# A program for one pattern of head flags behind a conditional: local heads score 11 blocks, and the Fourier transform stands ahead of a projection

## The chip, the cores and the metric

The kernel runs on one core of one Trainium2 chip. The metric is device microseconds of one execution, from the first to the last instruction of the program; of several runs the median counts. The core has TensorE (PE in the profile), VectorE (DVE), ScalarE (ACT), GpSimd (POOL) and SyncE (SP), which run their own instruction streams in order and wait for each other by semaphores; DMA queues move data beside them.

## The reference

Two layers follow each other. First, attention with 4 batches, 8 heads, 768 positions and 64 columns per head:

```python
scores = scale * q @ k.T                       # scale = 1/8
causal = rel >= 0                              # rel = query position - key position
stream = causal & ((key < 4) | (rel < 64))     # 4 sink keys and a window of 64
mask   = causal if is_retrieval[head] else stream
a      = softmax(where(mask, scores, -1e9))    # then a @ v
```

`is_retrieval` is an input; its value is [1, 0, 1, 0, 0, 0, 1, 0]. So heads 0, 2 and 6 are causal over everything before them ("retrieval heads") and the five others see the sink and the window alone ("local heads"). `n_sink` = 4 and `window` = 64 are known when the program is built.

Then the heads of a batch, side by side, form x (768 x 512), and a gated convolution follows:

```python
x1, x2, x3 = split(x @ w_proj, 3)              # w_proj 512 x 1536
conv = irfft(rfft(x2, axis=positions) * rfft(filter_fft, axis=positions))
out  = (x1 * conv * x3) @ w_out                # w_out 512 x 512
```

Output is 4 x 768 x 512 in float32.

## The kernel before

Work is cut into 16 pairs of heads, numbered n = 4 * batch + pair; the pair is heads 2p and 2p+1. Positions are cut into 6 tiles of 128. Names below are those of the operations in the kernel's own order; n is the pair, b the batch.

- **Loads and turns.** `lk`, `lq` and `lv` load float32; `ck`, `cq` cast q and k to bfloat16, `cv` casts v and places a column of ones beside it (`v_aug`). For n < 6 TensorE turns q and k (`T`, line 518) and `E` copies them out of PSUM; for the others a transposing DMA does it. `vf` (line 509, POOL) multiplies the values of far key tiles by a mask.
- **Scores.** A head has 21 blocks of 128 x 128 on or below the diagonal. For each pair they stand in 6 chunks (`sc`, line 542), which serve retrieval and local heads alike; the two heads of a pair use the lower and the upper 64 rows of TensorE. `ex` (line 561, ACT) takes the exponential out of PSUM. For n < 4 the mask is added in PSUM by a matmul with the identity (`sb`, line 555); for the others VectorE multiplies the exponentials by a mask (`mk`, line 571). Since the flags are data, masks and biases are made on the chip from the loaded flags (`lret`, `heads`, `code`, `mask`, `bias`, lines 350 to 388).
- **Attention.** `at` (line 580): 42 matmuls of 65 columns per pair; `rec` and `nm` (line 595) normalise; `tn`, `te` turn the result so that x stands with its columns on partitions (`xT`).
- **Convolution.** `x2` (line 633) projects; `xe`, `fa`, `fs` evict it and form the sum and the difference of the two halves of the positions (lines 645, 650); `X` (line 418) multiplies by the Fourier matrices `G`, 3 matmuls of 512 columns for each of 6 tiles; `Xe`, `pa`, `pb`, `pc` evict and multiply by the filter's spectrum (lines 664 to 674); `c` (line 716) transforms back, `ce`, `cv` (line 727) evict and join. `x1`, `x3` (line 691) project the gates, `xs`, `g`, `y` (lines 705 to 735) apply them, `o` (line 743) multiplies by `w_out`, `oe` evicts and `st` stores.
- **Order.** Nothing schedules at run time. The list `ORDER` names every operation once, with the PSUM slot (`@0` to `@3`, two banks each) that it takes and, for evictions, the engine (`/v`, `/s`, `/p` for DVE, ACT, POOL). Each engine's stream is that list, filtered.

At the start stand dummy matmuls (`blank`, line 221), and the Fourier matrices are made by sines on ACT.

## Time and profile before

Three runs took 212.41, 213.26 and 214.54 us; the median is 213.26. The profile is of one further execution:

| what | us |
|---|---|
| span of the profiled execution, its own time | 214.4 |
| PE busy | 196.3 |
| DVE busy | 177.8 |
| ACT busy | 141.9 |
| POOL busy | 58.1 |
| first exponential starts | 14.88 |
| last attention matmul ends | 169.80 |
| last eviction of the output ends | 211.08 |
| mean granted TensorE clock | 0.957 |

The profiled execution lies 1.1 us above the median of the runs and inside their spread; nothing of the program lies outside its span. Busy time counts an engine's instructions as one union of intervals. Matmuls are pipelined and their ends are modelled, so PE's busy time is longer than the pace at which it starts matmuls; the chain of work that ended last gives that pace, where PE runs without a gap. An instruction's duration on DVE and ACT overlaps the next one's by some 0.06 us.

### The profile page before, as it was taken

Reading aid. Unit: us, or ns where it says so; the run is one execution under the profiler, and the core shown is the slowest. Engines: PE = TensorE matmul, PEld = TensorE weight load, DVE = VectorE, ACT = ScalarE, POOL = GpSimd, SP = SyncE. Lnnn points to the kernel's source line nnn. Section 1 sums busy time; section 2 is a strip of 40 time slices with the busy share of each in tenths; the row PEclk is TensorE's granted clock in tenths of the full one; section 3 lists DMA queues with packets and bytes.
Section 4 is the critical chain, followed back from the end, with each engine's and each line's share of the span. In section 5 each row is a group of like instructions: output and inputs, shape, how many; then the busy total and the mean of one; then the engine's idle time right before and its main releaser. Section 6 shows DMA issues by size and latency. Waiting matters only on the chain.

```text
span 214.4 us, 4332 instructions
## 1 busy us (share of the span) xinstructions
PE 196.3 (92%) x1755; PEld 106.0 (49%) x1755; DVE 177.8 (83%) x287; ACT 141.9 (66%) x174; POOL 58.1 (27%) x79
## 2 busy tenths in 40 slices
PE   7486979899997999998999999999999999999992
PEld 2222547475355456444664564446544755555540
DVE  7379399866799879589999979999999995987951
ACT  7826785888995987996679867286779415334341
POOL 4283398066062002008534004082600000000000
PEclk9757696999999999999999999999999999999998
DMA  6799999979994047999999589999920560020436
GB/s 189 247 244 204 280 231 230 240 148 157 183 222 86 3 89 128 182 246 234 220 138 215 122 163 282 212 147 216 273 40 14 133 222 2 3 49 15 178 147 249
DMA packets 89764, 35.28 MB, mean 165 GB/s; under 512 B 80272, under 2 KB 86160, under 8 KB 89744
## 3 DMA queue, kind: packets, MB, share of 16 engines
q1 hardware_dynamic: 86848, 32.13, 67.6%
q0 software_dynamic: 2896, 2.88, 9.4%
q8 instruction: 13, 0.21, 0.4%
q14 instruction: 7, 0.06, 0.1%
HBM read 24.65 MB, written 6.29 MB: 144 GB/s over the span
## 4 chain that ended last, share of the span: by engine, by line
PE 51%; DVE 32%; ACT 7%; DMA 4%; issue 3%; POOL 1%; SPq 1%; ACTq 0%; POOLq 0%
PE x_ps L691 11%; PE out_ps L743 9%; PE x_ps L633 6%; DVE pT L571 5%; PE sc L542 5%; PE c_ps L716 5%; PE att L580 5%; ACT pT L561 4%; PE X_ps L418 4%; DMA ret_i<-in_is_retrieval_dram 4%; DVE attn L595 3%; DVE bias L382 2%; PE F_ps L418 2%; PE sc L555 2%; DVE x2s L174 2%
## 5 line engine op out<-in xcount | busy, mean ns | idle before, releaser
L561 ACT ACTIVATE pT<-sc 128x1024 bf16<-128x1024 f32 (+2 forms) x96 | 83.1, 921 | 21.6 <-PE sc L555 10.2
L691 PE MATMUL x_ps<-xT,wproj 128*128 128x384 bf16 x256 | 47.6, 326 | 2.0 <-DVE x1s L174 1.4
L542 PE MATMUL sc<-qkT 64*128 64x512 bf16 (+3 forms) x256 | 30.2, 322 | 4.9 <-DVE qkT L174 1.6
L691 PEld LDWEIGHTS <-wproj 128*128 128x128 bf16 x256 | 23.8, 98 | 21.8 <-issue 6.2
L571 DVE TENSOR_TENSOR pT<-pT,mask 128x1024 bf16<-128x1024 bf16 x37 | 31.1, 862 | 2.0 <-ACT pT L561 1.8
L493 POOL CAST qk_bf<-qk_f 128x768 bf16<-128x768 f32 x15 | 15.4, 1041 | 43.2 <-DMA qk_f<-in_q_dram 35.6
L504 POOL CAST v_aug<-v_f 128x768 bf16<-128x768 f32 x16 | 14.6, 918 | 40.7 <-DMA v_f<-in_v_dram 17.2
L580 PEld LDWEIGHTS <-pT 128*128 128x128 bf16 x672 | 23.8, 100 | 3.6 <-issue 0.9
L580 PE MATMUL att<-v_aug,pT 128*128 128x65 bf16 x352 | 24.8, 197 | 0.2 <-DVE pT L571 0.2
L743 PE MATMUL out_ps<-wout,gy 128*128 128x512 bf16 x96 | 23.2, 379 | 0.3 <-DVE gy L705 0.3
L633 PE MATMUL x_ps<-wproj,xT 128*128 128x512 bf16 x96 | 22.7, 380 | 0.0
L580 PE MATMUL att<-v_far,pT 128*128 128x65 bf16 x320 | 21.6, 196 | 0.0
L542 PEld LDWEIGHTS <-qkT 64*128 64x128 bf16 x256 | 9.6, 95 | 22.0 <-issue 15.6
L716 PE MATMUL c_ps<-Gi,P 128*128 128x384 bf16 x96 | 18.9, 326 | 1.6 <-DVE gy L705 1.3
L509 POOL TENSOR_TENSOR v_far<-v_aug,vmask 128x520 bf16<-128x520 bf16 x16 | 19.2, 1205 | 0.7
L176 ACT COPY o<-out_ps 128x1024 f32<-128x1024 f32 (+1 forms) x12 | 10.8, 911 | 10.9 <-PE out_ps L743 9.6
L418 PE MATMUL X_ps<-x,G 128*128 128x512 bf16 x72 | 18.0, 379 | 0.0
L727 DVE TENSOR_TENSOR conv<-evs,c_ps 128x384 bf16<-128x384 f32 x32 | 16.3, 548 | 1.6 <-ACT evs L176 1.3
L595 DVE TENSOR_TENSOR attn<-att,rec 128x768 bf16<-128x768 f32 x16 | 15.3, 954 | 0.6 <-DMA xT<-attn 0.2
L174 DVE COPY qkT<-qkT_ps 128x768 bf16<-128x768 bf16 x11 | 10.4, 953 | 6.2 <-PE qkT_ps L518 6.1
L176 ACT CAST x1s<-x_ps 128x768 bf16<-128x768 f32 x13 | 10.4, 805 | 7.7 <-PE x_ps L691 7.7
L176 ACT CAST x2s<-x_ps 128x1024 bf16<-128x1024 f32 x9 | 9.2, 1022 | 9.4 <-PE x_ps L633 9.0
(94 smaller groups left out, 245.9 us busy)
## 6 DMA issues: line engine op xcount, KB each, us to landing
qk_f<-in_k_dram SPq DMA_DIRECT2D x16, 384.0 KB, 6.6
qk_f<-in_q_dram SPq DMA_DIRECT2D x16, 384.0 KB, 6.3
v_f<-in_v_dram SPq DMA_DIRECT2D x16, 384.0 KB, 5.8
out_dram<-o SPq DMA_DIRECT2D x9, 512.0 KB, 3.3
wproj<-in_moe_w_proj_dram POOLq DMA_DIRECT2D x3, 512.0 KB, 7.2
out_dram<-o SPq DMA_DIRECT2D x6, 256.0 KB, 2.2
Xw<-X SPq DMA_DIRECT2D x8, 128.0 KB, 2.5
filt<-in_moe_filter_fft_dram POOLq DMA_DIRECT2D x1, 768.0 KB, 12.5
```

The costliest lines, as they stand in the source:

```text
L176: nc.scalar.copy(out=out, in_=in_)
L418: nc.tensor.matmul(ps[:, u, :], lhsT=matrix()[:, tile_no, m, :], rhs=src()[:, r, m, :], start=(m == 0), stop=(m == NM - 1))
L509: nc.gpsimd.tensor_mul(v_far(n), v_aug(n)[:, 0:4], vmask()[:, hp, :, :, None].to_broadcast([128, 4, 2, 65]))
L542: nc.tensor.matmul(sc[:, hh, m * 128:(m + cnt) * 128], lhsT=qkT(n)[rows, 1, j * 128:(j + 1) * 128], rhs=qkT(n)[rows, 0, i * 128:(i + cnt) ...
L561: nc.scalar.activation(out=pT(n)[:, :, c, 0:w], in_=held[f"sc.{n}.{c}"][:, :, 0:w], func=AF.Exp, scale=SCALE)
L571: nc.vector.tensor_mul(near, near, which)
L580: nc.tensor.matmul(att[:, hh, 65 * i:65 * i + 65], lhsT=pT(n)[:, hh, c, 128 * m:128 * m + 128], rhs=(v_far(n) if i >= j + 2 else v_aug(n)) ...
L595: nc.vector.tensor_mul(attn(n).rearrange("p i hh d -> p hh i d"), rows[:, :, :, 0:64], held[f"rec.{n}"][:, :, :, None].to_broadcast([128, ...
L633: nc.tensor.matmul(ps[:, half, :], lhsT=xT(b)[:, cc, half * HS + m * 128:half * HS + (m + 1) * 128], rhs=wproj()[:, cc, DM:2 * DM], start= ...
L691: nc.tensor.matmul(ps[:, s, 0:HS], lhsT=wproj()[:, cc, part * DM + cb * 128:part * DM + (cb + 1) * 128], rhs=xT(b)[:, cc, s * HS:s * HS + HS],
L716: nc.tensor.matmul(ps[:, r, 0:HS], lhsT=P(b)[:, t, u, ch], rhs=Gi()[:, tile_no], start=(m == 0), stop=(m == 2))
L743: nc.tensor.matmul(ps[:, i % 2, :], lhsT=gy(b)[:, cb, i * 128:(i + 1) * 128], rhs=wout()[:, cb, :], start=(cb == 0), stop=(cb == NC - 1))
```

## The change

The old program is kept whole as `general`. In front of it stands a short common part: it loads the eight flags to one partition, loads q and k of the first pair, compares the flags with one wanted pattern on VectorE, and reads the answer into a register of every engine. If the flags differ, `general` runs; otherwise a new program, `patterned`, which is built for heads 0, 2 and 6 being retrieval heads.

`patterned` differs in these ways:

- Pairs are heads c and c+4, taken in the order c = 2, 1, 0, 3. So in each batch one pair is two retrieval heads (RR), one is mixed (RL), and two are local (LL).
- A local head scores 11 blocks: 6 on the diagonal, and 5 blocks X, each of which holds the 4 sink keys and the last 64 keys of the tile before. For i = 1 that is tile 0 itself; for the others `kz`, `kx`, `ks` gather the keys, and `vx`, `vs` the values. `vf` is gone. LL has 3 chunks of scores in place of 6.
- Masks are constants (`mtab`, made by POOL), and biases one table (`btab`). The three loads of `w_proj` become six, with rows in the order of the new pairs.
- The Fourier transform is applied to the attention's output before the projection. Per pair `fd`, `fe` form difference and sum of the halves; for n >= 8 `fA`, `fS`, `fb`, `fr` go one step further, to sixths. `W` multiplies by `G` (for each of the two, 3 matmuls of 384 columns, or in sixths 2 of 256 and 1 of 128), `We` evicts 768 columns. `X` is then the projection of the transformed data: 4 matmuls of 512 columns for each of 6 tiles. `x2`, `xe`, `fa`, `fs` and the transform after the projection are gone.
- The back transform's matrices are made by TensorE (`Gt`, `Ge`), not by a DMA; q and k are turned by TensorE for n < 8; attention's outputs always (`tn`), where 7 went by DMA before. v, and q and k from n = 8, are loaded by head, in two DMAs each.
- More operations may go to any engine: `two` puts elementwise work on DVE or POOL, and `ev` can use POOL. The order is a new list, `FAST`.

The diff's core (the new order is cut, as are definitions that `patterned` repeats from `general` unchanged):

```diff
+TURNED = 8
+SIXTHS = (8, 9, 10, 11, 12, 13, 14, 15)
+TURNED_BACK = (0, 1, 2, 3, 4, 5, 6, 7, 8, 9, 10, 11, 12, 13, 14, 15)
+AHEAD = 1
+PAIRS = (2, 1, 0, 3)
+BIASED_FAST = 4
+FAST = """
+fcol0 mtab0 ck0/s lk2 lq2 ident cq0/s lq1 table tcol mblank fcol1 T0.1@0 lv0 sin0 blank2@1 angle2 E0.1/s tfrac
+mtab3 quarter lv1 turns2 T0.0 angle0 turns1 blank1@2 lk1 mtab2 E0.0/v ck2/s lq3 blank0@3 lv2 turns0 wrap2 cq2/s
...
+def _near():
+    out = []
+    for i in range(6):
+        if i:
+            out.append((0, "X", i, i, 1))
+        out.append((0, "B", i, i, 1))
+    return out
...
+SHAPES = {
+    "RR": [[[(hh, "B", j, i, cnt) for _, j, i, cnt in _runs(blocks)] for hh in range(2)] for blocks in CHUNKS],
+    "LL": [[_slot(NEAR[4 * c:4 * c + 4], hh) for hh in range(2)] for c in range(3)],
+    "RL": [
+        [_slot(NEAR[0:4], 1), [(0,) + d for d in _DIAG[0:2]]],
...
+KINDS = ("RL", "LL", "RR", "LL")
...
+    def ev(out, in_):
+        if now["engine"] == "v":
+            nc.vector.tensor_copy(out=out, in_=in_)
+        elif now["engine"] == "p":
+            nc.gpsimd.tensor_copy(out=out, in_=in_)
+        else:
+            nc.scalar.copy(out=out, in_=in_)
+
+    def two(out, a, b, op):
+        (nc.gpsimd if now["engine"] == "p" else nc.vector).tensor_tensor(out, a, b, op)
...
+            @op(f"vx{n}")
+            def _(n=n, which=which):
+                ev(v_x(n)[64:128, :, which], v_aug(n)[64:128, 1:5, which])
...
+            @op(f"kx{n}")
+            def _(n=n, at=at):
+                ev(kx(n)[at, :, 64:128], qkT(n)[at, 1].rearrange("r (n c) -> r n c", c=64)[:, 3:10:2])
...
+        @op(f"fd{n}")
+        def _(n=n):
+            x = attn(n).rearrange("p i hh d -> p i (hh d)")
+            two(fo(n)[:, 0], x[:, 0:NM], x[:, NM:NT], ALU.subtract)
...
+                if n in SIXTHS:
+                    nc.tensor.matmul(ps[:, u, 0:256], lhsT=br(n)[:, 1, u], rhs=G()[:, 3 * u:3 * u + 2, 0],
+                                     start=True, stop=False)
+                    nc.tensor.matmul(ps[:, u, 0:256], lhsT=uv(n)[:, 1 + 2 * u], rhs=Gk()[:, u],
+                                     start=False, stop=True)
+                    nc.tensor.matmul(ps[:, u, 256:384], lhsT=br(n)[:, 0, u], rhs=G()[:, 3 * u + 2, 0],
+                                     start=True, stop=True)
+                else:
+                    for m in range(NM):
+                        nc.tensor.matmul(ps[:, u, 0:HS], lhsT=fo(n)[:, u, m], rhs=G()[:, 3 * u:3 * u + 3, m],
+                                         start=(m == 0), stop=(m == NM - 1))
...
+                    for cc in range(NC):
+                        nc.tensor.matmul(ps[:, u, :], lhsT=xh(b)[:, cc, chain, 128 * part:128 * part + 128],
+                                         rhs=wproj()[:, cc, DM:2 * DM], start=(cc == 0), stop=(cc == NC - 1))
...
+    nc.sync.dma_start(out=flags, in_=is_retrieval[None, :])
...
+    nc.vector.tensor_scalar(out=zeros, in0=flags.bitcast(I32), scalar1=0.0, scalar2=None, op0=ALU.is_equal)
+    nc.vector.tensor_mul(local, zeros[:, 0:2 * H:2], zeros[:, 1:2 * H:2])
+    nc.vector.tensor_tensor(differs, local, want, ALU.not_equal)
+    nc.vector.tensor_reduce(out=other, in_=differs, op=ALU.max, axis=mybir.AxisListType.X)
+    reg = nc.values_load(other[0:1, 0:1], min_val=0, max_val=1)
+    with tc.If(reg != 0, preferred_fallthrough_block=False) as cmp:
+        general(tc, ahead, q, k, v, is_retrieval, n_sink, window, moe_w_proj, moe_filter_fft, moe_w_out, out)
+    with cmp.Else():
+        patterned(tc, ahead, pre, q, k, v, int(n_sink), int(window), moe_w_proj, moe_filter_fft, moe_w_out, out)
```

In the built program `patterned` stands directly behind the branch, `general` behind `patterned`, and the closing barrier behind `general`; so every engine jumps over `general` at the end.

## The prediction, made before the changed kernel was run

> **What bounds the kernel now.** First the page's list of engines:
>
> ```profile
> PE 196.3 (92%) x1755; PEld 106.0 (49%) x1755; DVE 177.8 (83%) x287; ACT 141.9 (66%) x174; POOL 58.1 (27%) x79
> ```
>
> PE looks full. The second view, the page's chain of work that ended last, puts less of the span on it:
>
> ```profile
> PE 51%; DVE 32%; ACT 7%; DMA 4%; issue 3%; POOL 1%; SPq 1%; ACTq 0%; POOLq 0%
> ```
>
> So two engines share the bound. Third, the table of windows, cut at the first exponential and at the last attention matmul:
>
> ```profile
> 0.00:14.88 14.88, 10.67 (x47) 4.45 (x47) 8.98 (x21) 8.44 (x13) 6.94 (x24) 0.78 0.79 230
> 14.88:169.80 154.92, 145.01 (x1488) 80.26 (x1487) 136.15 (x210) 119.01 (x143) 51.13 (x56) 0.97 0.91 175
> 169.80:214.41 44.61, 40.61 (x224) 21.34 (x222) 32.70 (x58) 14.45 (x19) 0.00 (x0) 0.99 0.31 105
> ```
>
> After the window and its length come PE, PEld, DVE, ACT, POOL. There are three stages: a head of 14.9 us; a middle of 154.9 in which DVE is busy 88%; a tail of 44.6. Fourth, the chain in order of time shows what carries the tail (start, us, what):
>
> ```profile
> 182.51 1.94 PE X_ps L418 x9
> ...
> 190.30 3.25 PE x_ps L691 x20
> 193.55 2.59 PE out_ps L743 x12
> 196.14 1.95 PE c_ps L716 x12
> ```
>
> The tail is PE without a gap, and it gives PE's true prices: 0.216 us for 512 columns, 0.163 for 384 (3.25/20, 1.95/12).
>
> **PE, part by part.** By such prices the old program's matmuls cost 170 us, dummies left out: attention's 672 at 0.0305 (1.28 us for 42) are 20.5; scores 17.1 (the chain has 8 matmuls, three chunks for both heads, in 0.60 us, so 0.05 per pair of blocks, times 336); biases 5.4; `x2` and `X` 36.3 (168 of 512 columns); the rest is unchanged or small.
> - Scores: 16 x (21 + 11) / 2 = 256 pairs of blocks, -4.0. The trace doesn't show how 128-column matmuls of two heads overlap: nearest rows are 0.05 a pair if they do and 0.07 a matmul if they don't (4.6 us for 64), up to +6 for the 252 of them. I take the first, since the long ones overlap fully.
> - Attention 472 matmuls for 672: -6.1. Biases (18 x 128, 5 x 384, 10 x 512 columns): -1.4.
> - `X` is 96 x 0.216 = 20.7, and the transform ahead 12.1 (48 x 0.163, and 16 sets of 0.27): 32.8 for 36.3, -3.5. Filter 24 to 18 matmuls: -1.3.
> - Transposes at 0.057 to 0.073: q and k +24, results +42, `Gt` 18: +4.9. They replace 10 DMA transposes, so DMA, 91% busy in the middle, is relieved. Loads by head add 32 issues of 0.45 us to SP's queue and `w_proj` three of 0.79 to POOL's; I cost SP's at nothing, since it mostly waits for buffers. Without that cover v would come late, and `cv` and `at` with it.
>
> PE: 170 - 11 = 159.
>
> **ACT.** Exponentials: 44 x 0.99, 16 x 0.82, 4 x 0.60 and 4 small, 61 for 86. Evictions and casts moved to it (9 `E` for 1, 11 casts for 5, 6 of v, 11 `We` for 9 `xe`, 5 more `ce`, 5 more `te`), a third table load (1.28) and `nm5` as 12 small ones: +37. ACT goes from 142 to 154.
>
> **DVE.** Removed, by the groups' busy time: mask and bias tables 15; `fa`, `fs`, `x2` evictions 14; mask products 31 to 23 (28,032 columns for 37,888); moved elsewhere (`ce`, 4 `E`, 7 `y`, filter scaling and others) 20. Added: `fd`, `fe` and the sixths 12; `We` 5; `kx`, `vx`, `v_aug` 8; constants, flags, other evictions 7. 178 - 57 + 32 = 153.
>
> To that comes POOL. The timeline of the two engines (start, us, instruction):
>
> ```profile
> 95.72 0.69 DVE L571 TENSOR_TENSOR pT<-pT,mask 128x1024 bf16<-128x1024 bf16 x1
> ...
> 99.64 1.53 DVE L571 TENSOR_TENSOR pT<-pT,mask 128x1024 bf16<-128x1024 bf16 x1
> ```
> ```profile
> 98.16 1.28 POOL L493 CAST qk_bf<-qk_f 128x768 bf16<-128x768 f32 x1
> 99.40 1.22 POOL L509 TENSOR_TENSOR v_far<-v_aug,vmask 128x520 bf16<-128x520 bf16 x1
> ```
>
> The same product takes 0.69 us alone and 1.53 beside POOL's. Over all groups DVE's times exceed their undisturbed ones by 17 us, for 49 us of POOL work on SBUF: 0.35 us each. The new POOL work is 60 us: 15 `fd`/`fe` of 384 and 9 gate products of 768 columns at `v_far`'s 2.0 ns a column, 3 of 1024, 13 of 256, 15 copies for v, 14 casts. At 0.35 that is 21, of which 9 are in the 153: DVE becomes 165. Between 153 (no extra) and 177 (the 0.55 of the 97 to 101 us stretch, 2.1 us lost in 3.8) I take the mean rate, since the new POOL operations are as long as the old (about 0.9 us).
>
> The Trainium skill (SBUF — State Buffer, Who interferes with whom) says that the port which the two engines share goes to one instruction for its whole length and the other engine's waits. The trace agrees (0.69 against 1.53). By that rule a DVE operation that reads PSUM with one SBUF input stays free, and the 0.94 to 0.96 us of every `nm` beside POOL bear it out.
>
> **Head.** Before the branch only the flags and two loads are issued; everything else on all engines stands behind the register. No row has a register load or a branch. Above, the bound is the old flags' load, 8.0 us from issue to landing; below, 0.8, when the engines start now. I take 5: a load lands after about 2.2 (shortest row of DMA issues) from 0.8, four small DVE operations of 0.2, and 1 us for register and branch. This delays the second pair's loads by some 3 us. Then ACT, in order: three table loads 3.8, four casts 3.3, `turns` 1.8, three `E` 2.5, sines 2.9: 14.4, and 1.5 of waits on loads and PE's 17 dummies. First exponential at **21** (14.9 before), 17 to 25 by the bounds. What hid the old setup, waits for loads, no longer hides this.
>
> **Tail.** Behind the last attention matmul PE still has 18 gate projections of four (11.7), `X` 5.2, 12 back transforms (5.9), two batches of `o` (10.4), `W` and transposes 2.3: **35.5** for 40.7. DVE has about 26 there, ACT 13. Then 3.9 us for the last eviction, store and barrier, as now, and one jump over `general`: instruction fetches show as 13 packets on the page, 1.07 us each; the store's landing (2.2) hides part. I take 1.1, between 0 and 3: **5.0**.
>
> The Trainium skill (Runtime: NRT & Kernel Launch, Instruction fetch mechanics) says that a taken branch to a far target stalls for a fetch of that block. No run here shows it; by it the jump costs, and the fall into `patterned` doesn't.
>
> **Middle.** DVE 165 - 9.5 (head) - 26 (tail) = 129.5. It filled 88% of the old middle, and 96% of 130 to 170 us (38.50 of 40). PE has 119, ACT 128, both level with it, which speaks against 96%: I take 91%, **142.5**. The ends, 135 and 147 to 155, make the range.
>
> **Sum.** 21 + 142.5 + 35.5 + 5.0 = 204 against the profiled 214.4. The runs' median is 0.5% under that execution, so **203** against 213.26.
>
> **Rivals.**
> - **ACT becomes the bound.** It gains 12 us while the others lose, and its stream has evictions on which PE's four slots wait. For: the middle's ACT load is 154 - 13 - 13 = 128, and it filled only 77% (119.0 of 154.9). At 84%: 152, sum 213.5, median **212.4**, no change. Against: its idle time now is mostly waiting on PE. Chance 0.12.
> - **POOL's port makes it slower.** Place: mask products and spectrum products of the middle, with POOL's gate and sum operations beside them. At 0.55 us of DVE per us of POOL: DVE 177, middle (177 - 35.5)/0.91 = 155.5, and at the old 88% 161: 217 to 222, median about **218**. It decides from 0.5 on, where the middle is 153. For: stretches like 97 to 101 us. Against: the mean is 0.35. Chance 0.13.
> - **The pattern isn't recognised**, and `general` runs: 214.4 + 5 + 1, median **219**. Flags 0, 2, 6 are what `want` holds. Chance 0.01.
> - **The forecast**, 195 to 210: chance 0.74.
>
> From these: faster by over 1% 0.76, within 1% 0.11, slower by over 1% 0.13; 1% is about what a measurement of this kernel can tell from none. Range for 8 in 10: 195 to 214, which takes in DVE's better filling, a head of 25 us and the ACT case.
>
> **What would show it.** First exponential near 21 us; the branch done near 5. Exponentials 61 us, ACT busy near 154, DVE near 165, POOL near 70, PE's tail near 35 us without gaps. Mask products beside POOL longer than 1 us mean the lock; mean ratios over 1.6 the slower rival. A head beyond 25 us, score matmuls of 128 columns above 0.07, or idle DVE waiting for ACT's `E` and `We` in the middle would make the number wrong.

## The result and the profile after

The changed kernel takes **206.63 us** in the median of six executions (205.25 to 210.22), the kernel before 213.9 in the median of six: ratio **0.965**, 95% interval 0.958 to 0.972. A ratio here and below counts only executions within 1.5% of the quickest of their kernel; medians are of all. The profiled execution has a span of 205.4 us, against 214.4 before. Forecast were 203 (195 to 214) and, for the span, 204. Time and span are not the same: over all executions on record the time is 1.4 to 3.3 us longer than the span (207.14 for the 205.4 here). The profiled execution of the kernel before, with its span of 214.4, was therefore longer than its three first runs and not inside their spread; the medians differ by 7.3 us where the two profiles differ by 9.0.

The engines in the page of the changed kernel, busy us, share of the span and instructions:

```profile
PE 183.4 (89%) x1718; PEld 107.1 (52%) x1718; DVE 161.0 (78%) x296; ACT 143.8 (70%) x199; POOL 81.5 (40%) x106
```

TensorE loses 13 us and VectorE 17, ScalarE gains 2, GpSimd 23. The chain of work that ended last, by engine:

```profile
PE 63%; ACT 16%; DVE 15%; issue 2%; DMA 1%; ACTq 0%; DVEq 0%
```

Before, it was PE 51% and DVE 32%. VectorE's share has halved; what that is worth is asked below. The windows, cut as before at the first exponential and at the last attention matmul (length, then PE, PEld, DVE, ACT, POOL, granted clock, DMA share, GB/s):

```profile
0.00:18.88 18.88, 10.28 (x67) 5.53 (x68) 10.22 (x29) 13.29 (x18) 10.58 (x28) 0.98 0.96 278
18.88:163.91 145.03, 137.04 (x1444) 82.11 (x1444) 121.97 (x223) 117.06 (x162) 57.24 (x68) 0.97 0.75 166
163.91:205.42 41.51, 36.04 (x211) 19.44 (x207) 28.77 (x46) 13.50 (x19) 13.68 (x12) 0.96 0.24 85
```

So the head costs 4.0 us more (18.9 for 14.9), the middle 9.9 less (145.0 for 154.9), the tail 3.1 less (41.5 for 44.6): 9.0 in all. In the middle TensorE has 8.0 us less to do than before (137.0 for 145.0), VectorE 14.2 less (122.0 for 136.2). TensorE is busy 94% of the middle in both kernels, VectorE 88% before and 84% now.

Each pair of heads has one reciprocal (`rec`), which dates the progress of the attention. The sixth starts at 69.3 us in both profiles, so all of the 9.0 us arise behind it. The stretch from the sixth to the last reciprocal, first of the kernel before, then of the changed one:

```profile
69.28:169.95 100.67, 97.66 (x951) 53.27 (x950) 91.36 (x140) 76.41 (x94) 24.77 (x23) 1.00 0.86 162
69.30:163.96 94.66, 91.46 (x933) 54.27 (x933) 88.60 (x171) 74.72 (x100) 35.01 (x39) 1.00 0.63 145
```

It is 6.0 us shorter, and TensorE has 6.2 us less to do in it. TensorE is busy 97% of it in both kernels; VectorE's share rises, from 91% to 94%.

The middle of the changed kernel is not one stage. A finer cut shows it:

```profile
55.00:79.62 24.62, 21.89 (x213) 12.07 (x210) 20.76 (x35) 19.62 (x34) 6.84 (x7) 1.00 0.71 148
79.62:144.75 65.13, 64.35 (x656) 38.03 (x657) 59.88 (x117) 52.05 (x70) 23.56 (x28) 1.00 0.70 155
144.75:153.61 8.86, 8.76 (x89) 4.66 (x88) 8.51 (x18) 7.88 (x10) 3.86 (x4) 1.00 0.06 19
```

From 79.6 to 144.8 us TensorE is busy 99% of the time and VectorE 92%; then for nine us VectorE is 96% busy, and TensorE still 99%. The chain in order of time names one of the two nearly full engines at each moment. Two cuts of it (start, us, what), the first from the long stretch, the second from the nine us:

```profile
101.81 1.28 PE f_att L1449 x42
103.09 0.34 PE f_xt_ps L1522 x6
103.42 3.45 PE f_X_ps L1553 x16
106.88 0.88 PE f_sc L1385 x7
...
146.80 0.95 DVE f_attn L1466
147.98 0.69 DVE f_m L974
```

Apart from two ScalarE steps (84.8 to 85.8 and 88.9 to 89.8 us) the chain is PE from 79.6 to 144.8, with attention, transposes and `X` back to back at 0.0305 (1.28/42), 0.057 and 0.216 (3.45/16) us each. From 144.8 to 153.6 it leads through ScalarE (1.5 us) and then VectorE. That doesn't make VectorE alone the bound there: in the same nine us TensorE started its matmuls without a gap of more than 0.1 us, so both engines were full. The tail looks alike. Its chain leads through ScalarE and VectorE in places, but the window row below it shows TensorE busy nearly throughout:

```profile
168.76 0.37 DVE f_uv L974
169.13 0.47 DVE f_conv L1629
169.65 3.42 PE f_x_ps L1588 x20
...
189.58 0.48 ACT f_evs L971
190.12 0.49 ACT f_evs L971
190.65 1.14 PE f_c_ps L1618 x6
...
200.28 0.59 ACT f_o L971
```
```profile
163.91:200.28 36.37, 36.04 (x211) 19.44 (x207) 28.77 (x46) 12.91 (x18) 13.68 (x12) 1.00 0.21 74
```

Between 163.9 and 200.3 us some 5.7 us of the chain are evictions and joins on ScalarE and VectorE (up to 166.5, 167.6 to 169.65 and 189.6 to 190.65). TensorE had other work in that time: by the starts of its matmuls under 1 us of the 36.4 is lost.

### The profile page after: what moved, and what is told of

Read it like the earlier page. It is cut to its first block, busy times and chain, and to the rows that moved or that the text cites. A ratio compares the mean times of both kernels' runs of the same rounds, so it can differ in the third digit from the quotient of the medians.

```text
span 205.4 us, 4423 instructions
## 1 busy us (share of the span) xinstructions
PE 183.4 (89%) x1718; PEld 107.1 (52%) x1718; DVE 161.0 (78%) x296; ACT 143.8 (70%) x199; POOL 81.5 (40%) x106
## 4 chain that ended last, share of the span: by engine, by line
PE 63%; ACT 16%; DVE 15%; issue 2%; DMA 1%; ACTq 0%; DVEq 0%
PE f_x_ps L1588 15%; PE f_X_ps L1553 10%; PE f_out_ps L1645 9%; PE f_c_ps L1618 7%; PE f_sc L1385 6%; ACT f_pT L1404 5%; PE f_att L1449 4%; PE f_blank_ps L1010 3%; DVE f_attn L1466 3%; PE f_qkT_ps L1340 2%; ACT f_qkT L971 2%; DVE f_fo L974 2%; ACT f_HAB L1205 2%; PE f_xt_ps L1522 2%; PE f_W_ps L1510 2%
## 5 line engine op out<-in xcount | busy, mean ns | idle before, releaser
L1404 ACT ACTIVATE f_pT<-f_sc 128x1024 bf16<-128x1024 f32 (+3 forms) x68 | 59.8, 921 | 7.2 <-PE f_sc L1385 5.1
L1588 PE MATMUL f_x_ps<-f_xT,f_wproj 128*128 128x384 bf16 x256 | 48.3, 327 | 1.0 <-ACT f_pT L1404 0.5
L1588 PEld LDWEIGHTS <-f_wproj 128*128 128x128 bf16 x256 | 23.1, 98 | 17.7 <-issue 2.6
L1385 PE MATMUL f_sc<-f_qkT 64*128 64x128 bf16 (+3 forms) x248 | 23.1, 258 | 1.9 <-DVE f_attn L1466 0.9
L1645 PE MATMUL f_out_ps<-f_wout,f_gy 128*128 128x512 bf16 x96 | 22.9, 380 | 0.0
L1553 PE MATMUL f_X_ps<-f_wproj,f_xh 128*128 128x512 bf16 x96 | 22.7, 380 | 0.0
L974 POOL TENSOR_TENSOR f_gy<-f_conv,f_gy 128x768 bf16<-128x768 bf16 x7 | 11.5, 1668 | 22.9 <-issue 13.2
L1629 DVE TENSOR_TENSOR f_conv<-f_evs,f_c_ps 128x384 bf16<-128x384 f32 x32 | 16.4, 548 | 3.2 <-ACT f_evs L971 2.0
L1449 PEld LDWEIGHTS <-f_pT 128*128 128x128 bf16 x472 | 17.5, 101 | 2.5 <-DVE f_attn L1466 0.6
L1385 PEld LDWEIGHTS <-f_qkT 64*128 64x128 bf16 x248 | 10.4, 95 | 15.8 <-issue 12.3
L1618 PE MATMUL f_c_ps<-f_Gi,f_P 128*128 128x384 bf16 x96 | 18.2, 325 | 0.4 <-ACT f_evs L971 0.2
L1449 PE MATMUL f_att<-f_v_aug,f_pT 128*128 128x65 bf16 x392 | 18.2, 199 | 0.2 <-DVE f_attn L1466 0.2
L971 ACT CAST f_x1s<-f_x_ps 128x768 bf16<-128x768 f32 x14 | 11.3, 810 | 8.2 <-PE f_x_ps L1588 6.5
L969 POOL COPY f_v_x<-f_v_aug 64x520 bf16<-64x520 bf16 (+1 forms) x15 | 9.7, 648 | 18.5 <-ACT f_v_aug L971 11.0
L1645 PEld LDWEIGHTS <-f_gy 128*128 128x128 bf16 x96 | 8.9, 98 | 10.2 <-issue 0.3
```

The source lines that it names most:

```text
L971: nc.scalar.copy(out=out, in_=in_)
L974: (nc.gpsimd if now["engine"] == "p" else nc.vector).tensor_tensor(out, a, b, op)
L1385: nc.tensor.matmul(sc[:, bank, col:col + 128 * cnt], lhsT=keys, rhs=qkT(n)[rows, 0, 128 * i:128 * (i + cnt)], start=(col == 0 or not biase ...
L1404: nc.scalar.activation(out=pT(n)[:, c, :, 0:w], in_=held[f"sc.{n}.{c}"][:, :, 0:w], func=AF.Exp, scale=SCALE)
L1449: nc.tensor.matmul(att[:, hh, 65 * i:65 * i + 65], lhsT=pT(n)[:, c, bank, col:col + 128], rhs=values, start=(z == 0), stop=(z == len(here) ...
L1553: nc.tensor.matmul(ps[:, u, :], lhsT=xh(b)[:, cc, chain, 128 * part:128 * part + 128], rhs=wproj()[:, cc, DM:2 * DM], start=(cc == 0), sto ...
```

## The experiments

Twelve runs follow; one of them (e5) is the changed kernel again. The questions were: what does the conditional cost and where; which engine carries the middle, before and after; and what sets the first 65 us.

### The conditional taken out (e1_nobranch)

```diff
-    reg = nc.values_load(other[0:1, 0:1], min_val=0, max_val=1)
-    with tc.If(reg != 0, preferred_fallthrough_block=False) as cmp:
-        general(tc, ahead, q, k, v, is_retrieval, ...)
-    with cmp.Else():
-        patterned(tc, ahead, pre, q, k, v, ...)
+    patterned(tc, ahead, pre, q, k, v, ...)
```

> The new program called directly: the flags aren't loaded, there is no comparison, no register, no branch, and the general program isn't built (so it would be wrong for other flags). Theory: the front is a serial price. In the changed kernel ACT starts at 3.40 us and DVE at 3.73, where they start at 0.8 without a branch; with the jump at the end gone too the span falls from 205.4 by 2.5 to 4.0 us, to 201.5 to 203, ratio to the kernel before 0.945 to 0.953. Rival: the first pair's loads (landing near 4.5 us) set the head anyway, and the ratio stays within 0.005 of 0.965.

Measured: ratio 0.956 (0.952 to 0.961), span 202.5. Against the changed kernel's 0.965, and 0.968 in its second measurement below, the conditional costs about 1%, some 2 us; against the second profile of the changed kernel (203.4), whose first 65 us went alike, 0.9 us. The span is in the range expected of a price paid in series, the ratio is above it, and the rival (within 0.005 of 0.965) didn't come either. Where it is paid is seen at both ends. The timeline of the first instruction of ScalarE (start, us, instruction, and in brackets how long it had waited and for what), first of this kernel:

```profile
0.81 1.28 ACT L971 ACT_TABLE_LOAD   x1 [0.81 <-PEq L1728]
```

and of the changed kernel:

```profile
3.40 1.28 ACT L971 ACT_TABLE_LOAD   x1 [3.40 <-DVE other L1726]
```

ScalarE starts 2.6 us earlier without the conditional. But then its first cast waits 1.9 us for the load of k,

```profile
3.98 0.83 ACT L971 CAST f_qk_bf<-qk_ahead 128x768 bf16<-128x768 f32 x1 [1.89 <-DMA qk_ahead<-in_k_dram]
```

and starts at 3.98, in the changed kernel at 4.69. The sixth reciprocal starts at 67.5 us, and in the second profile of the unaltered kernel at 67.4: at the front nothing was won. At the end, the last step of the chain without the conditional

```profile
198.49 0.59 ACT f_o L971
```

is 4.0 us ahead of the end of the span (202.49), as in the kernel before (210.49 to 214.41). In the changed kernel the same step starts at 200.28, 5.1 us ahead of it, and in its second profile at 198.39, 5.0 ahead. The jump over `general` costs **1.0 us**, which nothing covers. The DMA queues that fetch instructions show it: behind 199.5 us the changed kernel has (queue, packets, MB, share of 16 engines)

```profile
q14 instruction: 5, 0.04, 2.0%
q8 instruction: 1, 0.02, 1.0%
```

and the kernel without the conditional has no packet of these queues in its last five us, nor has the kernel before.

### The old program behind the conditional (e2_general)

```diff
-        if kind == "R":
+        if kind == "L":
             nc.vector.memset(want[:, h:h + 1], 0.0)
```

> The wanted pattern is inverted, so the comparison fails and the old program runs behind the front. Theory: the old program pays for the front (about 2.6 us of start) and for a taken branch into code that lies behind the other program; ratio 1.010 to 1.030, first instruction of the old program not before 5 us. Rival: the old program's head is bound by the landing of its flags at 10.3 us and by the mask tables, and the front is hidden: ratio 0.995 to 1.008.

Measured: 219.8 us, ratio 1.023 (1.020 to 1.026). This is the price of the conditional on a pattern that isn't the wanted one. Here the branch is taken, to a target far behind. The last comparison on VectorE ends at 2.95 us; then the timeline of this kernel shows the first instructions of GpSimd and VectorE:

```profile
4.16 0.14 POOL L310 IOTA tcol<- 128x3 f32 x1 [3.64 <-issue]
7.39 0.06 DVE L342 MEMSET quarter<- 128x1 f32 x1 [4.44 <-issue]
```

In the changed kernel, where the branch falls through, the comparison ends at 2.77 and the same engines start at:

```profile
3.58 0.35 POOL L1027 IOTA f_fcol<- 128x256 f32 x1 [3.07 <-DVE other L1726]
3.73 0.81 DVE L1061 MEMSET f_mtab<- 128x896 bf16 x1 [0.97 <-DVE other L1726]
```

So VectorE is 1.0 us behind the comparison if it falls through and 4.4 us if it jumps, GpSimd 0.8 and 1.2. In the first 8 us of this kernel the instruction queues move

```profile
q8 instruction: 1, 0.02, 1.6%
q14 instruction: 4, 0.03, 1.3%
```

all started between 4.7 and 4.9 us, the last done at 6.9, half a microsecond ahead of VectorE's first instruction. The changed kernel fetches nothing there: between 0.1 and 24.6 us its trace has no packet of these queues. The Trainium skill (Runtime: NRT & Kernel Launch, Instruction fetch mechanics) says that a taken branch to a target outside the prefetched window stalls for a fetch. The 3.5 us more on VectorE and the packets agree with that. GpSimd started at 4.16, ahead of the packets; why it needed none of them no run here shows.

### The head shortened: sine table ahead of the flags, and no dummies (e3_sinpre, e4_noblank, e6_both)

```diff
+    warm = pool.tile([1, 1], FP32, name="warm")
+    nc.vector.memset(warm, 0.0)
+    nc.scalar.activation(out=warm, in_=warm, func=AF.Sin)
     nc.vector.memset(want, 1.0)
```
```diff
-    for i, count in enumerate((8, 3, 6)):
+    for i, count in ():
```

The first edit is e3, the second (with the three names struck from the order) e4, both together e6.

> A sine on one element of ACT stands in the common part, ahead of the register, so that its table load lies beside the wait for the flags; the load before the first cast and the one before the first sine are gone. Theory: ACT's in-order chain to the first exponential loses 2 x 1.28 us; first exponential from 18.9 to 16.5 to 17.5 us and the span down by 1 to 2 us, ratio 0.955 to 0.960. Rival: PE's dummy matmuls, which end at 12.91, hold the second pair's transposes and with them the first exponential: nothing gained, ratio 0.963 to 0.967.

> The 17 dummy matmuls of the new program are left out (no part of the result). Theory: they stand on the chain from 6.44 to 9.00 and 9.64 to 12.91 us, so scores and transposes come some 3 us earlier; the first exponential comes 0.5 to 1.5 us earlier, the span falls by as much, ratio 0.958 to 0.963. Rival: without them the granted clock is lower in the following 15 us, where PE becomes the bound, and the span grows by 1 to 3 us, ratio 0.970 to 0.980.

> Both head edits together: the sine ahead of the branch and no dummy matmuls. Theory: each alone won 0.4 to 0.6 us because the other cover was still there (with the early table, the third turn waited for the dummies until 12.25 us; without dummies, the second turn waited for ACT, which stood in a table load until 7.8). Together the first exponential falls from 18.9 to 15 to 16.5 us and the span by 1.5 to 3 us; ratio lower than the changed kernel's by 0.007 to 0.014. Rival: loads of the second pair (casts at 9.4 and 10.7 us) hold the chain, and it stays within 1 us of 18.9; or the colder clock gives it back and the ratio is level or higher.

Measured: ratios 0.970 (0.965 to 0.976), 0.963 (0.959 to 0.967) and 0.969 (0.961 to 0.976), so none of them differs from the changed kernel. The gains expected of e3 and e6 didn't come; e4's 0.963 is at the edge of what was expected and within the scatter. The first exponential did come earlier (18.3, 18.5, 16.5 us for 18.9), and it paid nothing: in e6 the sixth reciprocal starts at 71.6 us, later than the unaltered kernel's 69.3 and 67.4. The chain of e6 in order of time shows what took its place:

```profile
18.61 16.13 DMA f_qk_f<-in_q_dram
34.74 0.02 issue
34.76 0.85 DVE f_qk_bf L967
```

A load of q for one of the first pairs, issued at 18.6, lands at 34.7, 16 us later, and TensorE has nothing to do from 33.0 to 36.5. The DMA engines are full here: their share is 1.2 between 18.5 and 28.5 us in the changed kernel (the row is shown below). A shorter head meets the loads. In e4 it is the same: a load of q issued at 18.9 lands at 35.6, and TensorE waits from 32.2 to 37.1.

### The unaltered kernel again (e5_again)

> The changed kernel itself, unaltered, beside the next three on the same chip, so that they can be compared with it and not only with the kernel before. Every theory: ratio 0.958 to 0.972 as measured first, span 205 to 207 us.

Measured: ratio 0.968 (0.961 to 0.976); span 203.4, 2.0 us shorter than the first profile of the same instructions and below the 205 to 207 expected. This pair of profiles is the cleanest view of what varies. The window in which they part, first profile of the changed kernel:

```profile
18.50:28.50 10.00, 8.97 (x91) 6.68 (x92) 4.74 (x10) 7.51 (x10) 6.12 (x12) 0.51 1.20 239
```

second profile:

```profile
18.50:28.50 10.00, 9.89 (x116) 6.77 (x115) 5.67 (x13) 7.96 (x10) 6.19 (x12) 0.66 1.18 235
```

The third number from the right is the granted TensorE clock. By the clock's own entries in the trace it is at half from 18.1 to 28.4 us in the first, in the second from 18.9 to 25.7. In the same ten us TensorE gets through 91 and 116 matmuls. The kernel before has the same, in three stretches (8.3 to 15.2, 18.6 to 25.4 and 32.2 to 35.6; the rows are of 8.0 to 18.5 and 18.5 to 28.5):

```profile
8.00:18.50 10.50, 7.57 (x44) 3.53 (x44) 7.09 (x15) 5.83 (x7) 7.66 (x14) 0.67 1.01 252
18.50:28.50 10.00, 8.57 (x92) 4.73 (x92) 6.70 (x11) 6.64 (x9) 3.44 (x5) 0.66 1.05 263
```

TensorE runs at half pace at the start too, though the column shows 1.00 there. The first six dummies of 512 columns in the changed kernel,

```profile
6.44 2.56 PE f_blank_ps L1010 x6
```

take 0.427 us each, twice the 0.216 of later; the clock's first entry in the trace is its rise to full, at 11.3. Over the profiles the picture is this (us; the fall of the clock at the very end of the span, with little or nothing left to compute, is left out):

| kernel | half pace from the start to | half clock later | first exponential | sixth reciprocal | last reciprocal | span |
|---|---|---|---|---|---|---|
| before | 4.9 | 6.8 + 6.8 + 3.4 | 14.9 | 69.3 | 170.0 | 214.4 |
| changed | 11.3 | 10.2 | 18.9 | 69.3 | 164.0 | 205.4 |
| again (e5) | 8.7 | 6.8 | 17.7 | 67.4 | 162.1 | 203.4 |
| no conditional (e1) | 8.7 | 6.8 | 17.7 | 67.5 | 162.2 | 202.5 |
| sine ahead (e3) | 10.4 | 10.2 + 3.4 | 18.3 | 70.9 | 165.6 | 206.8 |
| no dummies (e4, its longest execution) | 22.5 | 6.8 | 18.5 | 73.6 | 168.3 | 209.9 |
| both (e6) | 13.1 | 10.2 + 3.4 | 16.5 | 71.6 | 166.3 | 207.7 |
| late weights (e10, below) | 10.0 | 10.2 + 3.4 | 18.7 | 70.5 | 165.1 | 206.5 |

From the sixth reciprocal to the last all seven kernels with the new program take 94.6 to 94.7 us. All the difference arises ahead of it, and it goes with the time at half clock: start and later stretches together are 15.5, 15.6, 21.6, 23.6, 24.0, 26.8 and 29.3 us, and the sixth reciprocal comes at 67.4, 67.5, 69.3, 70.5, 70.9, 71.6 and 73.6. The later stretches last 3.4, 6.8 or 10.2 us, and each 3.4 loses 1.7 us of TensorE. Which is cause and which effect isn't always plain: in e4 and e6 TensorE also waited for a load. The windows of 3.41 us around the fall, in the first profile of the changed kernel:

```profile
11.18:14.59 3.41, 3.06 (x25) 1.40 (x24) 2.89 (x6) 1.28 (x3) 0.69 (x1) 1.00 1.17 314
14.59:18.00 3.41, 1.57 (x24) 1.32 (x23) 1.76 (x5) 3.39 (x6) 3.04 (x6) 1.00 1.15 353
18.00:21.41 3.41, 2.00 (x18) 1.35 (x15) 1.36 (x2) 3.30 (x4) 3.41 (x8) 0.52 1.18 287
21.41:24.82 3.41, 3.41 (x22) 1.73 (x23) 2.31 (x7) 2.30 (x3) 2.81 (x5) 0.50 1.22 199
```

The clock falls behind a window in which TensorE was busy 46% (1.57 of 3.41), stays low behind one with 59% (2.00 of 3.41), and is back at 28.4, after TensorE has been full. In the second profile the window ahead of the fall holds 1.11 us of TensorE, in e6's second fall 0.48, in e4, where without the dummies the fall moved to 36.2, nothing. The Trainium skill (TensorE: Matmul & The Clock Gate, Part 1) tells of a clock gate that looks at windows of 3.4 us, goes to half after an idle one and back to full after a busy one. The lengths here agree; that the window has to be idle does not, since half a window of work was too little here. With windows of 3.41 us laid end to end from the clock's own entries over all fourteen profiles, every window at full clock with TensorE busy up to 45% was followed by half clock, none above 60% was, and between them (46 to 60%) both happen. Where the threshold lies stays open in that range. Over timed executions the mean clock of the two kernels (its entries alone, without the start) is much the same (0.957 to 0.984 before, 0.960 to 0.983 after), so it explains the scatter and not the gain.

### TensorE made dearer in the changed kernel (e7_new_pe8)

```diff
-                    for cc in range(NC):
+                    for z, cc in enumerate([0] * (2 if b < 3 else 0) + list(range(NC)), -2 if b < 3 else 0):
                         nc.tensor.matmul(ps[:, u, :], lhsT=xh(b)[:, cc, chain, 128 * part:128 * part + 128],
                                          rhs=wproj()[:, cc, DM:2 * DM], start=(z <= 0), stop=(z < 0 or z == NC - 1))
```

> The changed kernel with two more matmuls of 512 columns in each projection tile X of batches 0 to 2 (the first product twice more, overwritten): 36 x 0.216 = 7.8 us more PE work before the last attention matmul's stage ends, none on other engines. Theory: PE carries the middle from 55 us on (63% of the chain), so 5.5 to 8 us longer, ratio up by 0.026 to 0.037 over the unaltered one. Rival, as the prediction had it (DVE the bound of the middle): 1 to 3 us.

Measured: ratio 1.000 (0.996 to 1.004), 6.8 us over e5's on the same chip for a dose of 7.8 (36 matmuls of 0.216). Of the dose 24 matmuls, 5.2 us, fall behind the sixth reciprocal, and the stretch of 94.7 us becomes 100.0. There TensorE's work comes through whole. The whole profile is 8.5 us longer than the first of the changed kernel, with the same time at half clock.

### VectorE made dearer in the changed kernel (e8_new_dve8, e9_new_dve_small)

```diff
+    scr = sb.tile([128, 64], FP32, name="scr", tag="scr")
+    dosed = {form % n for n in range(3, 12) for form in ('at%d.1', 'W%d.1')}
...
+        if name in dosed:
+            nc.vector.reciprocal(out=scr, in_=scr)
```

The first of the two had 384 columns for 64.

> The changed kernel with 18 more VectorE operations (reciprocals of a scratch tile, 384 columns, about 0.46 us each, no POOL port in question, no reader) behind attention and transform of pairs 3 to 11: 8.3 us more DVE work in the middle. Theory (PE carries, DVE busy 84% of the middle): 1.5 to 4 us longer, ratio up by 0.007 to 0.019. Rival, as the prediction had it (DVE the bound): 6 to 8 us, 0.028 to 0.037.

Measured: ratio 1.134 (1.126 to 1.143). The dose was far larger than meant: 0.46 us each was put down without a row for it, since the kernel's own reciprocals have 12 columns (0.22 us). The row of the dosed tile in e8, durations in ns as least, median and greatest:

```profile
L1683 DVE RECIPROCAL scr<-scr x18: 2482/2544/2554, 40.9 to 166.9; 128x384 f32<-128x384 f32 x18
```

That is 45.7 us in place of 8, of which some 36 came through. So large a dose makes any engine the bound and tells nothing of a small one. It was repeated with 64 columns.

> The changed kernel with 18 extra VectorE instructions (reciprocal of a 128x64 tile) between pairs 3 and 11, two per pair. The 384-column ones of the run before took 2.54 us each, 6.6 ns a column, so these are put at 0.45 us each by the same price per column: 8 us in all. Theory A (the middle is carried by TensorE, VectorE 84% busy in it has some 20 us of gaps): a third or less comes through, +1 to +3 us, ratio to the kernel before 0.97 to 0.98. Theory B (VectorE carries the middle, as the prediction had it): 6 to 8 us come through, ratio 0.995 to 1.005.

```profile
L1683 DVE RECIPROCAL scr<-scr x18: 486/544/554, 44.7 to 134.7; 128x64 f32<-128x64 f32 x18
```

The dose is 9.7 us (18 x 0.54). Measured: ratio 0.971 (0.965 to 0.976), which is 0.002 to 0.006 over the two measurements of the changed kernel: 0.5 to 1.3 us, a tenth of the dose, with an uncertainty of nearly 2 us. By time, VectorE doesn't seem to carry the middle. Its profile says less: it is 4.1 us longer than the first of the changed kernel (209.5 for 205.4), at nearly the same time at half clock (20.7 for 21.6 us, start included). 14 of the 18 (7.5 us) lie behind the sixth reciprocal, and 94.7 us become 97.6:

```profile
70.55:168.10 97.55, 91.71 (x927) 54.35 (x933) 94.09 (x185) 74.70 (x100) 35.23 (x39) 1.00 0.62 140
```

That is 2.9 us, or two fifths of what was put there. It was the longest of its executions; the six of them ran at a mean granted clock of 0.980, against 0.973 for the twelve of the changed kernel, which flatters the reading by time. So between a tenth and two fifths comes through.

### The same two doses in the kernel before (e11_old_pe8, e12_old_dve_small)

```diff
-        for m in range(NM):
+        more = name[0] == "X" and name[5] < "3"
+        for z, m in enumerate([0] * (2 if more else 0) + list(range(NM)), -2 if more else 0):
             nc.tensor.matmul(ps[:, u, :], lhsT=matrix()[:, tile_no, m, :], rhs=src()[:, r, m, :],
-                             start=(m == 0), stop=(m == NM - 1))
+                             start=(z <= 0), stop=(z < 0 or z == NM - 1))
```

The edit for VectorE is that of e9, with the scores' chunk 0 (`sc`) of each pair for `W`, which the old program lacks.

> The kernel before with 36 extra 128x512 matmuls (two more in each accumulation group of the transforms of the parts 0 to 2, adding to the sum's first term, so the output differs), about 7.8 us of TensorE, spread over the middle as in the same dose on the changed kernel, where 0.87 of it came through. If TensorE carried the middle of the kernel before as much as that of the changed one: +6 to +7 us, ratio 1.028 to 1.033. If it was shared with VectorE, as the chain of waits of before has it (PE 51%, DVE 32%): +3 to +5 us, ratio 1.014 to 1.023. If VectorE alone carried it: under +2 us, ratio below 1.01.

> The kernel before with the same 18 VectorE instructions (reciprocal of a 128x64 tile, 0.54 us each in the changed kernel, 9.7 us in all) between pairs 3 and 11. In the changed kernel some 0.4% (1 us) of them came through. If the change took the VectorE off the path (theory A: before, its chain of waits is DVE for 32%, VectorE 83% busy): 3 to 6 us come through, ratio 1.014 to 1.028. If TensorE alone carried the middle before as it does after (its dose of 7.8 us gave 1.0275): 0 to 2 us, ratio 1.000 to 1.009.

Measured: ratios 1.028 (1.022 to 1.033) and 1.039 (1.031 to 1.047). By medians both are 5.6 and 5.5 us over the kernel before (220.62 against 215.01, 220.76 against 215.26). The four doses side by side, as the part that came through in timed executions (by ratios, by medians; e9's median against that of e10, on the same chip):

| | kernel before | changed kernel |
|---|---|---|
| TensorE, 7.8 us | 5.9, 5.6 | 6.8, 7.7 |
| VectorE, 9.7 us | 8.4, 5.5 | 0.5 to 1.3, 1.5 |

VectorE's ratio is above what either theory expected, its median inside the 3 to 6 us of theory A. By time, then, VectorE's dose costs the kernel before several times what it costs the changed one. The profiles do not bear that out. The kernel before with VectorE's dose has a span of 218.3, 3.9 us over 214.4, at much the same time at half clock (23.4 and 22.0 us, start included); 11 of the 18 (6.0 us) lie behind the sixth reciprocal, and the stretch to the last one becomes 2.6 us longer, with 3.4 us of half clock in it:

```profile
70.36:173.61 103.25, 98.59 (x939) 53.41 (x950) 94.21 (x151) 76.52 (x93) 24.48 (x23) 0.98 0.81 158
```

So by profiles the same 9.7 us cost 3.9 before and 4.1 after. The clock accounts for much of the difference by time: e12's executions ran at a mean granted clock of 0.960, those of the kernel before beside them at 0.971; e9's at 0.980 for 0.973. An estimate: 0.011 of 215 us is 2.4 us, which leaves 3.1 of e12's 5.5 by medians; 0.007 of 205 is 1.5, which makes 2.5 to 3.0 of e9's 1.0 to 1.5. Whether the dose itself lowers the clock is not shown. That VectorE lost its hold on the middle through the change is therefore **not shown**.

TensorE's dose reads alike in every way. In e11 the stretch from the sixth to the last reciprocal becomes 106.6 us for 100.7, 6.0 more for the 6.9 (32 matmuls) that lie in it; in e7 it was 5.3 for 5.2. The ratio of e11 is at the lower end of what was expected if TensorE carried the middle of the kernel before as much as that of the changed one. So TensorE carried the middle in both kernels, and VectorE, nearly as busy, lets a part of its own added work through in both.

### The weights' loads put behind those of the early pairs (e10_late_weights)

```diff
-lk3 mtab1 wrap0 lw2.0 lq5 sc0.5@1
+lk3 mtab1 wrap0 lq5 sc0.5@1
...
-fe1/p rec2
+fe1/p lw2.0 lw2.1 lw0.0 lw0.1 rec2
```

> The changed kernel with four of the six loads of the projection's weights (1 MB of the 10.7 MB that move between 6 and 46 us) issued on POOL only behind the gate product of pair 1, near 42 us, instead of between 7 and 25 us; their first readers start near 60 us. Theory C (the stretch from the first exponential to the fourth reciprocal is bound by the landing of loads): 1 MB at the 268 GB/s of that window is 3.7 us less ahead of the early pairs' q, k and v, the sixth reciprocal comes 2 to 4 us earlier than 67 to 69 us and the ratio falls to 0.945 to 0.957. Rival D (the stretch is bound by the engines, the spread of it being chance): the sixth reciprocal stays within 1 us and the ratio between 0.963 and 0.970. A worse end is open: the moved loads collide with those of pairs 5 to 7 or land behind their readers, ratio above 0.975.

Measured: ratio 0.962 (0.957 to 0.968). The move did what it should to the loads: in its trace three loads of q and k that in the first profile of the changed kernel are issued at 24.9, 34.9 and 36.7 us and land at 37.8, 43.1 and 44.0 now land at 33.6, 36.1 and 37.5. The fourth reciprocal starts at 43.2 us for 43.6, the sixth at 70.5 for 69.3, where a second stretch of half clock (54.3 to 57.8) makes up for more than the difference. The ratio lies between what was expected of C and of D, the sixth reciprocal a little later than either has it. So the landing of loads doesn't set the pace of the unaltered kernel: rival D stands, within an uncertainty of 1 us. It does in the profiles with a shorter head, as the chain of e6 shows. Late weights together with a short head were not tried.

No version here is beyond doubt faster than the changed kernel with its conditional. The one without it (e1) comes nearest, by some 1%, with intervals that overlap, and it computes the right thing for a single pattern alone.

## Why the prediction was right, and where it was not

The time was right (206.6 in 195 to 214, and 205.4 of span against a sum of 204), but in good part by luck: the head came 2.1 us shorter and the middle 2.5 longer than forecast, and the middle was worked out on the wrong engine. The forecast's own sum for TensorE, 11 us less, with 1.1 for the jump, gives 204 as well (214.4 - 11 + 1.1), so the number doesn't tell the two accounts apart. Its steps:

- **What bounds the kernel before.** "Two engines share the bound" is right in part. Both doses came out at the end (e11, e12), but TensorE's for the most part and VectorE's, by the profiles, for two fifths.
- **PE, 170 to 159.** The prices held: 0.216 us for 512 columns (5.18/24), 0.163 for 384 (1.30/8), 0.0305 for attention (1.28/42). The price taken for 128-column scores, 0.025 a matmul (0.05 a pair), is low: the chain has 7 in 0.44 us, 14 in 0.50 and 16 in 0.62, so 0.036 to 0.06 with wider ones among them. For 252 matmuls that is some 3 us more at the least, still nearer to overlap than to the 0.07 of the other bound. Two sums are off as well: 472 blocks, one for each of the attention's matmuls, are 236 pairs and not 256 (1 us less), and 252 matmuls at 0.07 for 0.025 would have been 11 us more, not 6.
- **ACT, 154.** It measured 143.8. The exponentials are as said (44.4 + 13.2 + 2.4 + 1.6 = 61.6 by forms, 61 forecast). The term "+37" for evictions moved to it was mis-sized: 143.8 - 61.6 = 82.2 of other work, against 141.9 - 86.1 = 55.8 before, is +26.
- **DVE, 165.** It measured 161.0, by two errors that cancel. Without POOL's disturbance the sum was 144 (153 less the 9 in it); the groups of the changed kernel exceed their undisturbed instances by some 10 us in all (13.6 if every instance is held against the shortest of its line and shape), so about 151 is DVE's own work. The extra for POOL, 21 us at "0.35 each", was some 10 for 81.5 us of POOL work. The lock itself is there. The timeline of VectorE and of GpSimd in the changed kernel:

```profile
153.47 1.29 DVE L1431 TENSOR_TENSOR f_pT<-f_pT,f_mtab 128x512 bf16<-128x512 bf16 x1
```
```profile
152.36 2.12 POOL L974 TENSOR_TENSOR f_P<-f_P,f_m 128x1024 bf16<-128x1024 bf16 x1 [2.02 <-DVE f_P L974]
```

  A product that takes 0.41 us alone took 1.29 beside POOL's, as the rule of the Trainium skill (SBUF — State Buffer, Who interferes with whom) has it. But it met POOL less often: all twelve of 1024 columns ran undisturbed (0.677 to 0.692 us), and over all mask products the mean is 1.18 of the undisturbed (24.1 us for 20.5), against 1.26 before (0.862 for 0.686).
- **POOL, "near 70".** 81.5. `fd` and `fe` took 1.06 us in the mean for 0.78 estimated from columns, the gate products 1.67 for 1.55. A price per column, from one long row, leaves out what a short instruction costs besides.
- **Head, 21.** 18.9 and 17.7 in two profiles. Flags landed at 2.0 for 3.0, and engines started at 3.4 to 3.7 us, not near 5: a load of 64 bytes took 1.2 us, not the 2.2 of the shortest row on the page. "No longer hides this" was wrong: without the conditional the first cast waits for k until 3.98 us, and the sixth reciprocal comes no earlier (e1).
- **Tail, 35.5 + 5.0.** 36.4 (163.9 to 200.3) and 5.1. The ends are right in their parts too: 3.9 and a jump of 1.0 for 1.1 (e1). "Without gaps" holds: TensorE is busy 36.0 of the 36.4, though the chain leads through other engines for 5.7.
- **Middle, 142.5 — the step that failed.** It was DVE's work, 129.5 us, over a filling of 91%. Measured are 122.0 us over 84%, in 145.0: two errors that cancel. The forecast read DVE's 96% of 130 to 170 us as the sign of the bound; in that same window TensorE was busy 97%:

```profile
130.00:170.00 40.00, 38.82 (x371) 21.17 (x369) 38.50 (x58) 27.59 (x34) 11.71 (x11) 1.00 0.80 165
```

  TensorE carried the middle, before and after. Its dose (e7) came through by nine tenths and more, VectorE's (e9) by a tenth to two fifths, much the same as in the kernel before by the profiles. The forecast should have divided TensorE's busy time: it fills 94% of the middle in both kernels (145.0 of 154.9, 137.0 of 145.0).
- **From span to time.** The sum was lowered by 0.5%, to 203, because the runs' median of 213.26 was set against a span of 214.4. A time is longer than its span (207.14 for 205.4), so 204 of span stood for some 206 of time. That would have been nearer to the 206.6.

**The rivals.** ACT as the bound didn't come: it lies at 117 us of 145, and most of its 16% of the chain lies ahead of 91 us. POOL's port "decides from 0.5"; it was far below the 0.35 (some 10 us for 81.5, 0.12). The pattern not recognised was priced at 219 and measures 219.8 (e2).

**Where the 9 us are from.** Shown is that they arise behind the sixth reciprocal: 6.0 up to the last one and 3.0 behind it, the jump's 1.0 already paid. In the first of these TensorE has 6.2 us less to do, at 97% busy in both kernels, and the doses say that its work comes through there nearly whole (e7, e11). The medians of timed executions differ by 7.3 and 7.9, somewhat less than the two profiles. Which share the 11-block heads have, and which the transform ahead of the projection, was not separated.

## What to carry to other kernels

When two engines are both near nine tenths busy, a forecast needs to know which one is late, and neither busy shares nor the chain of work that ended last tell: the chain led through VectorE where TensorE had no gap. A small dose on each engine tells more, if it is sized from its own row and if the executions with and without it had the same granted clock; here the clock alone moved such a reading by 2 us. A conditional with the common case falling through cost 2.6 us of start, of which nothing was left at the sixth reciprocal, and 1.0 at the end, bare: a program that is kept for the rare case is best placed where the common one need not jump over it. And before a head is shortened, the landing of the loads behind it wants a look.

## What the runs showed of the hardware that was not expected

- The granted TensorE clock falls to half for 3.4, 6.8 or 10.2 us at a time, in every profile at least once in the first 60 us; it fell behind windows of 3.4 us in which TensorE was busy 0 to 60%, and behind every one with 45% or less. Two profiles of one kernel differ by one such stretch and by 2.0 us of span.
- Matmuls run at half pace from the start of the program (512 columns in 0.427 us, 0.216 later) until the clock's first entry in the trace, at 8.7 and 11.3 us in two profiles of the changed kernel and at 22.5 without the dummies; the granted clock of the rows reads 1.00 there.
- A reciprocal of 128 x 384 in float32 on VectorE takes 2.54 us, of 128 x 64 0.54: 6.3 ns a column between them, where a bfloat16 product of 1024 columns takes 0.68.
- Behind a taken branch to a far target VectorE began 4.4 us after the flags were compared, GpSimd 1.2; falling through, 1.0 and 0.8. Five packets of instructions were fetched between 4.7 and 6.9 us where the branch was taken, none where it fell through.
- A load of eight flags (64 bytes) took 1.2 us from issue to landing at the start, with the DMA queues nearly empty; loads of 192 and 384 KB of q, k and v issued between 18 and 20.2 us took 12.8 to 16.8 in the changed kernel.
